# Cosformer attention and a quick-GELU MLP on one core: the last 64 rows of k and v on 64 partitions with zeroed rows below, instead of packed on two partition halves

## The chip, the cores and the metric

The kernel runs on one core of a Trainium2 chip. The metric is the device time of one execution in microseconds: 302.57 us for the kernel before, the median of 3 runs (302.42 to 303.06). The profile is a separate execution on the same kind of core; its span is 300.8 us.

TensorE multiplies matrices into PSUM, VectorE and ScalarE prepare operands and copy results out of PSUM, GpSimd issues most of the loads and stores, and SyncE issues the transposes by DMA.

## What is computed

Linear attention with cosine weights, and then a two-layer MLP over all tokens:

```python
# q, k, v: 8 batches, 8 heads, 576 positions, 64 columns
def phi(x, c, s):
    r = np.maximum(x, 0.0)
    return np.concatenate([r * c, r * s], axis=-1)      # 128 columns
q_p, k_p = phi(q, cos_w, sin_w), phi(k, cos_w, sin_w)
kv  = np.einsum('bhsf,bhsd->bhfd', k_p, v)              # per head: (128 x 576) (576 x 64)
z   = np.sum(k_p, axis=2)
num = np.einsum('bhsf,bhfd->bhsd', q_p, kv)
den = np.einsum('bhsf,bhf->bhs', q_p, z)[..., None] + 1e-06
x   = (num / den), as 4608 tokens of 512
h   = x @ w_in                                          # 512 -> 2048
out = (h * sigmoid(1.702 * h)) @ w_out                  # 2048 -> 512, float32
```

The kernel computes in bf16 with sums in f32. It takes z along as a 65th column of v that holds ones.

## The kernel before

The 4608 tokens are nine blocks of 512. In block i TensorE does the two MLP products of its tokens (the first is L305, into `mm` tiles; the second L345), and between them the attention of batch i + 1: q' and k' are prepared on VectorE, k^T v is computed per head (`unit_kv`), then the products of q' with it (`unit_num`, L289), and the result is turned by DMA into `xT` for the next block.

The sum over the 576 positions is cut into chunks of rows on partitions. Batches 0 and 1 use six chunks of 96 rows. Batches 2 to 7 use four chunks of 128 rows and a tail of 64, chunk 4. The tail is packed: heads 0 to 3 lie on partitions 0 to 63, heads 4 to 7 on partitions 64 to 127.

```python
def load_tail(b, n, on=nc.gpsimd):
    if n == "q":
        t = state[b][n, 4] = two.tile([64, 512], BF16, name=n + "t")
        on.dma_start(out=t.rearrange("p (h d) -> p h d", h=H),
                     in_=SRC[n][b, :, 512:576, :].rearrange("h p d -> p h d"))
        return
    t = state[b][n, 4] = two.tile([128, 256], BF16, name=n + "t")
    for m in range(2):
        on.dma_start(out=t[64 * m:64 * m + 64].rearrange("p (h d) -> p h d", h=4),
                     in_=SRC[n][b, 4 * m:4 * m + 4, 512:576, :].rearrange("h p d -> p h d"))
# ... (cut)
def kv_half(b, n, kv):                                   # L250; batch 1
    r, last = (96, 5) if b < 2 else (128, 4)
    for h in range(4 * n, 4 * n + 4):
        for c in range(last + 1):
            nc.tensor.matmul(kv[:, ds(h % 4 * (D + 1), D + 1)], kp[:r, c, h, :], vt[:r, c, h, 0:D + 1],   # L254
                             start=(c == 0), stop=(c == last))

def kv_tiled(b, kv):                                     # L257; batches 2 to 7
    for h in range(4):
        o = [kv[:, n, ds(h * (D + 1), D + 1)] for n in range(2)]
        for n in range(2):
            for c in range(4):
                nc.tensor.matmul(o[n], kp[:, c, h + 4 * n, :], vt[:, c, h + 4 * n, 0:D + 1],              # L263
                                 start=(c == 0), stop=False)
        for n in range(2):
            r = slice(64 * n, 64 * n + 64)
            nc.tensor.matmul(o[n], kp[r, 4, h, :], vt[r, 4, h, 0:D + 1], start=False, stop=True)          # L266
# ... (cut)
def unit_kv(b):
    kvs_new(b)
    kv = at_tile()                                       # two PSUM banks, one for each half n
    if b < 2:
        for n in range(2):
            kv_half(b, n, kv[:, n])
    else:
        kv_tiled(b, kv)
    for n in range(2):
        kvs_half(b, n, kv[:, n])                         # L269: copy on VectorE to bf16
# ... (cut)
def mm2_last(i, t):                                      # the last 128 tokens
    yps = mm_tile()
    ysb = ypool.tile([128, d_model], F32, name="ysb")
    for n in range(2):
        cols = slice(0, 384) if n == 0 else slice(384, 512)
        w = 384 if n == 0 else 128
        if n == 1:
            yps = mm_tile()
        for fc in range(FC):
            nc.tensor.matmul(yps[:, 0:w], gT[fc][:, ds(t * 128, 128)], w_out_sb[:, fc, cols],             # L369
                             start=(fc == 0), stop=(fc == FC - 1))
        if n == 0:
            nc.scalar.copy(ysb[:, cols], yps[:, 0:w])                                                     # L372
        else:
            nc.vector.tensor_copy(ysb[:, cols], yps[:, 0:w])                                              # L374
        # ... (cut: two stores of 64 rows each, one from SyncE, one from ScalarE, L376)
# ... (cut)
warmup(11, mm_tile())        # L463: eleven idle matmuls between the last transposes of q' and batch 0's first k^T v
kv_lo, kv_hi = mm_tile(), mm_tile()
kv0(kv_lo, 0, 4)
```

Of the kernel before, what the change touches and what calls it, by code (L numbers as in the profile page):

```python
# [9 lines left out]
F32 = mybir.dt.float32  # L10
BF16 = mybir.dt.bfloat16
# [10 lines left out]
def kernel(  # L22
# [9 lines left out]
    nc = tc.nc  # L32
    B, H, S, D = q.shape
    d_model = H * D
# [9 lines left out]
    one = ctx.enter_context(tc.tile_pool(name="one", bufs=1))  # L44
    two = ctx.enter_context(tc.tile_pool(name="two", bufs=2))
# [8 lines left out]
    def rows(c):  # L54
        return 128 if c < 4 else 64

    def wide(b, n):
        return b < 2 and n != "q"

    def krows(b, c):  # L60
        return 96 if b < 2 else 128

    warm = const.tile([128, TB], BF16)
    nc.vector.memset(warm, 0.0)
# [13 lines left out]
    state = {b: {} for b in range(B)}  # L78
    SRC = {"q": q, "k": k, "v": v}
# [7 lines left out]
                     in_=SRC[n][b, h0:h1, 0:np_ * t, :].rearrange("h (p c) d -> p h (c d)", c=t))  # L87

    def load_tail(b, n, on=nc.gpsimd):
        if n == "q":  # L90
            t = state[b][n, 4] = two.tile([64, 512], BF16, name=n + "t")
            on.dma_start(out=t.rearrange("p (h d) -> p h d", h=H),
                         in_=SRC[n][b, :, 512:576, :].rearrange("h p d -> p h d"))
            return

        t = state[b][n, 4] = two.tile([128, 256], BF16, name=n + "t")
        for m in range(2):
            on.dma_start(out=t[64 * m:64 * m + 64].rearrange("p (h d) -> p h d", h=4),  # L98
                         in_=SRC[n][b, 4 * m:4 * m + 4, 512:576, :].rearrange("h p d -> p h d"))

    def load_all(b):
        for n in "qkv":
# [4 lines left out]
    w_out_sb = one.tile([128, FC, d_model], BF16)  # L107
# [9 lines left out]
    pos_i = const.tile([128, NC], I32)  # L117
# [4 lines left out]
    for n in range(2):  # L122
        nc.sync.dma_start(out=q0[:, ts(n, 1024)].rearrange("p (h e) -> p h e", h=4),
                          in_=q[0, 4 * n:4 * n + 4, 0:512, :].rearrange("h (p c) d -> p h (c d)", c=4))
    nc.gpsimd.iota(pos_i[:, 0:4], pattern=[[1, 4]], base=0, channel_multiplier=4)
    for m in range(2):
        nc.gpsimd.iota(pos_i[64 * m:64 * m + 64, 4:5], pattern=[[1, 1]], base=512, channel_multiplier=1)
    nc.gpsimd.iota(pos6_i, pattern=[[1, 6]], base=0, channel_multiplier=6)
    load_main(0, "k", 0, 4)
    nc.gpsimd.iota(id_i, pattern=[[1, 128]], base=0, channel_multiplier=-1)  # L130
# [31 lines left out]
    kp = one.tile([128, 6, H, 2 * D], BF16, name="kp")  # L162
    vt = one.tile([128, 6, H, VW], BF16, name="vt")
# [22 lines left out]
    def part(b, n, c, h0, h1):  # L186
        if wide(b, n):
            return state[b][n][:96, 0:48 * D].rearrange("p (h c d) -> p c h d", c=6, d=D)[:, c, h0:h1]
        if c == 4 and n != "q":
            return state[b][n, 4].rearrange("p (h d) -> p h d", d=D)  # L190
        if c == 4:
            return state[b][n, 4].rearrange("p (h d) -> p h d", d=D)[:, h0:h1]
        return state[b][n][:, 0:32 * D].rearrange("p (h c d) -> p c h d", c=4, d=D)[:, c, h0:h1]
# [7 lines left out]
    def qn_slot(b, c):  # L201

        return state[b]["qn4"] if b < 2 and c == 4 else state[b]["qn"][:rows(c), c]

    def prep(b, n, c, h0=0, h1=H, on=(nc.vector, nc.vector)):
        r = rows(c) if n == "q" else krows(b, c)
        for cs, w in enumerate((cos6, sin6) if wide(b, n) else (cosw, sinw)):
            o = qn_slot(b, c) if n == "q" else kp[:r, c]
            if n == "k" and c == 4 and b > 1:
                h1 = 4  # L210
            oc, i, wc = o[:, h0:h1, cs * D:cs * D + D], part(b, n, c, h0, h1), w[:r, c:c + 1]
            if on[cs] is nc.scalar:
                nc.scalar.activation(oc, i, AF.Relu, scale=wc)
            else:
                nc.vector.tensor_scalar(oc, i, 0.0, wc, op0=MAX, op1=MUL)  # L215
# [2 lines left out]
        nc.vector.tensor_copy(vt[:96, :, :, 0:D], state[b]["v"][:96, 0:48 * D].rearrange("p (h c d) -> p c h d", c=6, d=D))  # L218

    def prep_v(b, c, h0=0, h1=H):  # L220
        if c == 4:
            h1 = 4
        nc.vector.tensor_copy(vt[:krows(b, c), c, h0:h1, 0:D], part(b, "v", c, h0, h1))

    def q_slot(b, c):
# [24 lines left out]
    def kv_half(b, n, kv):  # L250
# [3 lines that stand above are left out]
                nc.tensor.matmul(kv[:, ds(h % 4 * (D + 1), D + 1)], kp[:r, c, h, :], vt[:r, c, h, 0:D + 1],  # L254
                                 start=(c == 0), stop=(c == last))

    def kv_tiled(b, kv):  # L257

        for h in range(4):
            o = [kv[:, n, ds(h * (D + 1), D + 1)] for n in range(2)]  # L260
            for n in range(2):
                for c in range(4):
                    nc.tensor.matmul(o[n], kp[:, c, h + 4 * n, :], vt[:, c, h + 4 * n, 0:D + 1], start=(c == 0), stop=False)  # L263
            for n in range(2):
                r = slice(64 * n, 64 * n + 64)
                nc.tensor.matmul(o[n], kp[r, 4, h, :], vt[r, 4, h, 0:D + 1], start=False, stop=True)  # L266

    def kvs_half(b, n, kv, copy=nc.vector.tensor_copy, w=D + 1):
        copy(state[b]["kvs"][:, n, :, 0:D + 1],  # L269
             kv[:, 0:4 * w].rearrange("p (h e) -> p h e", h=4)[:, :, 0:D + 1])  # L270
# [4 lines left out]
    def unit_kv(b):  # L275
        kvs_new(b)
        kv = at_tile()
        if b < 2:
            for n in range(2):
                kv_half(b, n, kv[:, n])  # L280
        else:
            kv_tiled(b, kv)
        for n in range(2):
            kvs_half(b, n, kv[:, n])

# [15 lines left out]
    gT = {}  # L301
# [57 lines left out]
    def mm2_last(i, t):  # L359

        yps = mm_tile()
        ysb = ypool.tile([128, d_model], F32, name="ysb")
        for n in range(2):
            cols = slice(0, 384) if n == 0 else slice(384, 512)
            w = 384 if n == 0 else 128
            if n == 1:
                yps = mm_tile()
            for fc in range(FC):
                nc.tensor.matmul(yps[:, 0:w], gT[fc][:, ds(t * 128, 128)], w_out_sb[:, fc, cols],  # L369
                                 start=(fc == 0), stop=(fc == FC - 1))  # L370
            if n == 0:
                nc.scalar.copy(ysb[:, cols], yps[:, 0:w])  # L372
            else:
                nc.vector.tensor_copy(ysb[:, cols], yps[:, 0:w])  # L374
            for m, (p0, cnt, row, step) in enumerate(pieces(i * 4 + t)):
                (nc.sync if m == 0 else nc.scalar).dma_start(out=out[row:row + (cnt - 1) * step + 1:step, cols],  # L376
                                                             in_=ysb[p0:p0 + cnt, cols])
# [123 lines left out]
    for i in range(NBLK):  # L501
        work = {n: [] for n in range(32)}
        b = i + 1

        def at(n, f, *a):
            work[n].append(lambda: f(*a))

        if b < B:
            if i == 0:
                at(13, unit_num, 0, 4)  # L510
                at(13, turn_x, 0, 4)
            k0, k1, ks = (11, 24, (25, 26, 27, 28)) if i == 0 else (0, 12, (17, 19, 21, 23, 25))
            at(k0, prep_new, b)
            if i == 1:

                at(0, prep, 1, "q", 4)
                at(0, turn_q, 1, 4)
                at(14, unit_num, 1, 4)
                at(14, turn_x, 1, 4)
            for c in range(4 if i == 0 else NC):  # L520
                at(k0, prep, b, "q", c)
                if i == 0:
                    at(22 + c // 2, turn_q_at, b, c, AC.copy)
                else:
                    at(k0 + c, turn_q, b, c)
            for c in range(6 if b < 2 else NC):
                at(20 if i == 0 else k1 - 4 + c // 2, prep, b, "k", c)
                if b >= 2:
                    at(k1 - 1, prep_v, b, c)
            if b == 1:  # L530
                at(k1 - 1, prep_v_wide, b)
            at(k1, unit_kv, b)
            for c, k in enumerate(ks):
                at(k, unit_num, b, c)
                if i == 0 and c < 4:
                    at(min(k + 2, 31), turn_x_at, b, c)
                else:
                    at(k, turn_x, b, c)
            if 0 < i and b + 1 < B:
                at(1, load_all, b + 1)  # L540
        for n in range(32):
            if n < FC:
                if i > 0 or n > 3:
                    mm1(i, n)
            elif i == 0:
                mm2(i, n % 4, (n - FC) // 4)
            elif i == NBLK - 1 and n >= 28:
                if n == 28:
                    mm2_last(i, 3)
            else:  # L550
                mm2(i, (n - FC) // 4, n % 4)
            for f in work[n]:
                f()
        if i == 0:
            evac(i, 3, nc.vector)
# [30 lines left out]
```

## Time and profile before

| what | value |
|---|---|
| time, median of 3 | 302.57 us |
| span of the profile | 300.8 us |
| TensorE busy | 292.1 us, 97% |
| VectorE, ScalarE, GpSimd busy | 35%, 42%, 34% |
| memory traffic | 36.70 MB read, 9.44 MB written |
| L263, full-depth k^T v matmuls | 192, mean 194 ns |
| L266, half-depth k^T v matmuls | 48, mean 200 ns |
| L254, batch 1's k^T v matmuls, 96 rows | 48, mean 193 ns |
| L369, last tile | 16 of 384 columns, mean 326 ns; 16 of 128, mean 219 ns |

The page of a profile gives the busy time of each engine, the same in 40 slices of the span with the TensorE clock that was granted, the transfers, the chain of work that ended last, and the costliest groups of instructions. Groups are named by the line of the kernel. The mean of a TensorE group is the time from the start of one matmul to its end; matmuls follow each other before the one ahead has ended, so that the distance between two starts, and not the mean, says what one more of them costs. The timeline view gives these starts. A busy share of TensorE near 100% says that the engine always had a matmul under way, and not that it took them in at its best rate.

### The profile page before, as it was taken

To read this page: it belongs to the slowest core of one execution; us is meant where nothing else is said; L and a number is where in the kernel's file an instruction comes from. 1 tells how busy PE (TensorE), PEld (TensorE's weight loads), DVE (VectorE), ACT (ScalarE), POOL (GpSimd) and SP (SyncE) were. 2 spreads that over 40 slices of the span, in tenths; PEclk is the share of its full clock that TensorE was granted. 3 is DMA by queue.
4 is the path that set the end of the run, shared out by engine and by line. 5 is a ranking of instruction groups with operands and counts; after the bars stand their busy time and mean duration, and the time that the engine had idled before them with its cause. 6 is when DMAs were issued, how large, how long until landed. Compare 5 with 4: busy or idle time off the path is not lost.

```text
span 300.8 us, 5168 instructions
## 1 busy us (share of the span) xinstructions
PE 292.1 (97%) x1985; PEld 149.6 (50%) x1985; DVE 104.2 (35%) x355; ACT 126.1 (42%) x215; POOL 101.1 (34%) x130
## 2 busy tenths in 40 slices
PE   8979999999999999999999999999999999999994
PEld 3665456545544554455445544554455444444443
DVE  5740544663590159015811482147313300000000
ACT  7736622663137312641165116511652156226511
POOL 8532231550268025700691159003501110020021
PEclk9979999999999999999999999999999999999999
DMA  7999999599989987994899969996901520011033
GB/s 186 188 204 198 202 198 186 162 137 177 179 161 154 183 118 152 176 184 97 120 186 157 140 128 174 148 166 114 193 2 35 113 72 1 35 70 37 0 67 74
DMA packets 87496, 39.66 MB, mean 132 GB/s; under 512 B 57328, under 2 KB 85232, under 8 KB 87472
## 3 DMA queue, kind: packets, MB, share of 16 engines
q0 software_dynamic: 41040, 27.01, 59.9%
q1 hardware_dynamic: 46272, 12.20, 25.6%
q8 instruction: 15, 0.25, 0.3%
q10 hardware_dynamic: 160, 0.13, 0.1%
q14 instruction: 9, 0.07, 0.1%
HBM read 36.70 MB, written 9.44 MB: 153 GB/s over the span
## 4 chain that ended last, share of the span: by engine, by line
PE 93%; DVE 3%; ACT 1%; DMA 1%; issue 0%; DVEq 0%; ACTq 0%
PE mm L305 40%; PE mm L345 39%; PE at L289 3%; PE at L263 3%; PE mm L441 2%; DMA q<-in_q_dram 1%; PE mm L369 1%; DVE qn L215 1%; PE at L266 1%; PE mm L397 1%; PE mm L75 1%; DVE xb L297 1%; ACT qT L236 1%; ACT xT L435 1%; PE at L254 0%; PE mm L388 0%
## 5 line engine op out<-in xcount | busy, mean ns | idle before, releaser
L345 PE MATMUL mm<-w_out_sb,g 128*128 128x512 bf16 x560 | 128.6, 379 | 0.0
L305 PE MATMUL mm<-xT,w_in_sb 128*128 128x512 bf16 (+1 forms) x564 | 123.7, 378 | 0.0
L310 ACT ACTIVATE g<-mm 128x512 bf16<-128x512 f32 x144 | 85.5, 598 | 50.3 <-PE mm L305 49.8
L357 POOL DMA_DIRECT2D out_dram<-ysb x54 | 49.6, 922 | 163.3 <-ACT ysb L355 158.7
L305 PEld LDWEIGHTS <-w_in_sb 128*128 128x128 bf16 x564 | 54.3, 98 | 64.3 <-issue 0.2
L345 PEld LDWEIGHTS <-g 128*128 128x128 bf16 x560 | 52.2, 98 | 56.9
L355 ACT COPY ysb<-mm 128x512 f32<-128x512 f32 x34 | 19.9, 586 | 97.7 <-PE mm L345 97.7
L269 DVE CAST kvs<-at 128x260 bf16<-128x260 f32 x14 | 5.4, 425 | 66.6 <-PE at L266 59.6
L297 DVE TENSOR_TENSOR xb<-at,inv 128x512 bf16<-128x512 f32 (+1 forms) x36 | 24.8, 689 | 1.2
L295 DVE TENSOR_SCALAR den<-at 128x8 f32<-128x8 f32 (+1 forms) x36 | 5.9, 164 | 44.5 <-PE at L289 44.5
L374 DVE COPY ysb<-mm 128x128 f32<-128x128 f32 x1 | 0.3, 291 | 59.4 <-PE mm L369 59.4
L289 PEld LDWEIGHTS <-qT 128*128 128x128 bf16 x272 | 13.0, 98 | 8.2 <-DVE xb L297 0.6
L215 DVE TENSOR_SCALAR qn<-q,cosw 128x512 bf16<-128x512 bf16 (+1 forms) x36 | 12.5, 352 | 10.8 <-DMA q<-in_q_dram 10.8
L289 PE MATMUL at<-kvs,qT 128*128 128x65 bf16 x272 | 14.2, 194 | 0.3
L215 DVE TENSOR_SCALAR qn<-q,sinw 128x512 bf16<-128x512 bf16 (+1 forms) x34 | 12.6, 369 | 0.0
L98 POOL DMA_DIRECT2D vt<-in_v_dram x12 | 7.6, 641 | 7.8 <-DMA out_dram<-ysb 3.1
L98 POOL DMA_DIRECT2D kt<-in_k_dram x12 | 8.8, 749 | 4.1 <-DMA v<-in_v_dram 2.3
L263 PE MATMUL at<-vt,kp 128*128 128x65 bf16 x192 | 9.9, 194 | 0.0
L86 POOL DMA_DIRECT2D v<-in_v_dram x10 | 8.3, 834 | 4.4 <-DMA w_in_sb<-in_moe_w_in_dram 2.5
L215 DVE TENSOR_SCALAR kp<-k,sinw 128x512 bf16<-128x512 bf16 x24 | 8.9, 371 | 0.0
L86 POOL DMA_DIRECT2D k<-in_k_dram x9 | 7.8, 865 | 3.0 <-ACT g L310 2.5
L263 PEld LDWEIGHTS <-kp 128*128 128x128 bf16 x192 | 7.6, 97 | 2.1
(78 smaller groups left out, 155.7 us busy)
## 6 DMA issues: line engine op xcount, KB each, us to landing
out_dram<-ysb POOLq DMA_DIRECT2D x38, 128.0 KB, 3.0
out_dram<-ysb POOLq DMA_DIRECT2D x16, 256.0 KB, 3.0
q<-in_q_dram POOLq DMA_DIRECT2D x7, 512.0 KB, 10.3
k<-in_k_dram POOLq DMA_DIRECT2D x6, 512.0 KB, 11.5
v<-in_v_dram POOLq DMA_DIRECT2D x6, 512.0 KB, 12.3
w_out_sb<-in_moe_w_out_dram POOLq DMA_DIRECT2D x4, 512.0 KB, 18.2
w_in_sb<-in_moe_w_in_dram POOLq DMA_DIRECT2D x3, 512.0 KB, 12.4
q<-in_q_dram SPq DMA_DIRECT2D x2, 512.0 KB, 4.3
```

The lines of the kernel that those rows point to most:

```text
L86: on.dma_start(out=state[b][n][:np_, t * D * h0:t * D * h1].rearrange("p (h e) -> p h e", h=h1 - h0), in_=SRC[n][b, h0:h1, 0:np_ * t, :].r ...
L98: on.dma_start(out=t[64 * m:64 * m + 64].rearrange("p (h d) -> p h d", h=4), in_=SRC[n][b, 4 * m:4 * m + 4, 512:576, :].rearrange("h p d - ...
L215: nc.vector.tensor_scalar(oc, i, 0.0, wc, op0=MAX, op1=MUL)
L263: nc.tensor.matmul(o[n], kp[:, c, h + 4 * n, :], vt[:, c, h + 4 * n, 0:D + 1], start=(c == 0), stop=False)
L289: nc.tensor.matmul(nm[:, h // 4, ds(h % 4 * (D + 1), D + 1)], q_slot(b, c)[:, h, :], state[b]["kvs"][:, h // 4, h % 4, 0:D + 1], start=Tru ...
L297: nc.vector.tensor_tensor(state[b]["xb"][:r, c].rearrange("p (n h) d -> p n h d", n=2), nm4[:, :, :, 0:D], inv[:r].unsqueeze(3).to_broadca ...
L305: nc.tensor.matmul(hps[:, c0:c1], w_in_sb[:, kc, ds(fc * 128, 128)], xT[:, kc, ds(i * TB + c0, c1 - c0)], start=(kc == 0), stop=(kc == KC ...
L310: nc.scalar.activation(g, hps, AF.Gelu_apprx_sigmoid)
L345: nc.tensor.matmul(yps, gT[fc][:, ds(t * 128, 128)], w_out_sb[:, fc, :], start=(fc == 0), stop=(fc == FC - 1))
L355: nc.scalar.copy(ysb, cur[t])
L357: nc.gpsimd.dma_start(out=out[row:row + (n - 1) * step + 1:step, :], in_=ysb[p0:p0 + n, :])
L441: nc.tensor.matmul(first[fc][:, c0:c1], w_in_sb[:, kc, ts(fc, 128)], xT[:, kc, c0:c1], start=(kc == 0), stop=(kc == KC - 1))
```

## The change

The tails of k and v go back to 64 partitions, with all eight heads side by side, one load for each tail instead of two. Rows 64 to 127 of chunk 4 of k' and v are zeroed once, in block 1, and the product of batches 2 to 7 then takes chunk 4 at full depth like the other four: each head is five matmuls of 128 rows, and the half-depth pairs are gone. The heads are computed half by half, as in batch 1. The number of matmuls is the same. Apart from that, the last output tile is cut into two halves of 256 columns instead of 384 and 128, and one small table of positions is made by one instruction instead of two. The eleven idle matmuls ahead of batch 0's k^T v, which the change's name mentions, stand in both kernels.

What it is for: to rid the k^T v product of the two forms of matmul and of the packed layout, at the price of matmuls that multiply zeros.

```diff
     def krows(b, c):
-        return 96 if b < 2 else 128
+        return 96 if b < 2 else rows(c)
# ... (cut)
     def load_tail(b, n, on=nc.gpsimd):
-        if n == "q":
-            t = state[b][n, 4] = two.tile([64, 512], BF16, name=n + "t")
-            ...
-        t = state[b][n, 4] = two.tile([128, 256], BF16, name=n + "t")
-        for m in range(2):
-            on.dma_start(out=t[64 * m:64 * m + 64].rearrange("p (h d) -> p h d", h=4),
-                         in_=SRC[n][b, 4 * m:4 * m + 4, 512:576, :].rearrange("h p d -> p h d"))
+        if on is nc.gpsimd:
+            t = two.tile([64, 512], BF16, name=n + "t")
+        else:
+            t = one.tile([64, 512], F32, name=f"{n}t{b}")
+        state[b][n, 4] = t
+        on.dma_start(out=t.rearrange("p (h d) -> p h d", h=H),
+                            in_=SRC[n][b, :, 512:576, :].rearrange("h p d -> p h d"))
# ... (cut)
-    for m in range(2):
-        nc.gpsimd.iota(pos_i[64 * m:64 * m + 64, 4:5], pattern=[[1, 1]], base=512, channel_multiplier=1)
+    nc.gpsimd.iota(pos_i[:, 4:5], pattern=[[1, 1]], base=512, channel_multiplier=1)
# ... (cut: part, prep and prep_v lose their special cases for chunk 4)
-    def kv_tiled(b, kv):
-        ... (cut: the function shown above)
# ... (cut)
         kv = at_tile()
-        if b < 2:
-            for n in range(2):
-                kv_half(b, n, kv[:, n])
-        else:
-            kv_tiled(b, kv)
+        for n in range(2):
+            kv_half(b, n, kv[:, n])
# ... (cut)
+        hd = d_model // 2
         for n in range(2):
-            cols = slice(0, 384) if n == 0 else slice(384, 512)
-            w = 384 if n == 0 else 128
+            cols = ds(n * hd, hd)
# ... (cut: w becomes hd in the matmul and the two copies)
             if i == 1:
+                at(2, nc.vector.memset, kp[64:128, 4], 0.0)
+                at(2, nc.vector.memset, vt[64:128, 4], 0.0)
```

More of the change, by code (lines that the diff above doesn't have):

```diff
@@ L89, in load_tail @@
     def load_tail(b, n, on=nc.gpsimd):
-        if n == "q":
-            t = state[b][n, 4] = two.tile([64, 512], BF16, name=n + "t")
-            on.dma_start(out=t.rearrange("p (h d) -> p h d", h=H),
-                         in_=SRC[n][b, :, 512:576, :].rearrange("h p d -> p h d"))
-            return
-        t = state[b][n, 4] = two.tile([128, 256], BF16, name=n + "t")
-        for m in range(2):
-            on.dma_start(out=t[64 * m:64 * m + 64].rearrange("p (h d) -> p h d", h=4),
-                         in_=SRC[n][b, 4 * m:4 * m + 4, 512:576, :].rearrange("h p d -> p h d"))
+        if on is nc.gpsimd:
[5 more added lines that the diff above has]
+                            in_=SRC[n][b, :, 512:576, :].rearrange("h p d -> p h d"))
     def load_all(b):
@@ L188, in part @@
             return state[b][n][:96, 0:48 * D].rearrange("p (h c d) -> p c h d", c=6, d=D)[:, c, h0:h1]
-        if c == 4 and n != "q":
-            return state[b][n, 4].rearrange("p (h d) -> p h d", d=D)
         if c == 4:
@@ L208, in prep @@
             o = qn_slot(b, c) if n == "q" else kp[:r, c]
-            if n == "k" and c == 4 and b > 1:
-                h1 = 4
             oc, i, wc = o[:, h0:h1, cs * D:cs * D + D], part(b, n, c, h0, h1), w[:r, c:c + 1]
@@ L220, in prep_v @@
     def prep_v(b, c, h0=0, h1=H):
-        if c == 4:
-            h1 = 4
         nc.vector.tensor_copy(vt[:krows(b, c), c, h0:h1, 0:D], part(b, "v", c, h0, h1))
@@ L255, in kv_half @@
                                  start=(c == 0), stop=(c == last))
-    def kv_tiled(b, kv):
-        for h in range(4):
-            o = [kv[:, n, ds(h * (D + 1), D + 1)] for n in range(2)]
-            for n in range(2):
[L262 to L266, printed above, removed]
     def kvs_half(b, n, kv, copy=nc.vector.tensor_copy, w=D + 1):
@@ L277, in unit_kv @@
         kv = at_tile()
-        if b < 2:
-            for n in range(2):
-                kv_half(b, n, kv[:, n])
-        else:
-            kv_tiled(b, kv)
+        for n in range(2):
+            kv_half(b, n, kv[:, n])
         for n in range(2):
@@ L368, in mm2_last @@
             for fc in range(FC):
-                nc.tensor.matmul(yps[:, 0:w], gT[fc][:, ds(t * 128, 128)], w_out_sb[:, fc, cols],
+                nc.tensor.matmul(yps[:, 0:hd], gT[fc][:, ds(t * 128, 128)], w_out_sb[:, fc, cols],
                                  start=(fc == 0), stop=(fc == FC - 1))
             if n == 0:
-                nc.scalar.copy(ysb[:, cols], yps[:, 0:w])
+                nc.scalar.copy(ysb[:, cols], yps[:, 0:hd])
             else:
-                nc.vector.tensor_copy(ysb[:, cols], yps[:, 0:w])
+                nc.vector.tensor_copy(ysb[:, cols], yps[:, 0:hd])
             for m, (p0, cnt, row, step) in enumerate(pieces(i * 4 + t)):
```

## The prediction

> **What bounds the kernel now.** I read the busy share in slices first, then the chain that ended last, then TensorE's timeline at the two kinds of k^T v, then the last microseconds. From the page: busy tenths of TensorE in 40 slices, the granted TensorE clock, and the chain by engine and by line:
>
> ```profile
> PE   8979999999999999999999999999999999999994
> ...
> PEclk9979999999999999999999999999999999999999
> ...
> PE 93%; DVE 3%; ACT 1%; DMA 1%; issue 0%; DVEq 0%; ACTq 0%
> PE mm L305 40%; PE mm L345 39%; PE at L289 3%; PE at L263 3%; PE mm L441 2%; DMA q<-in_q_dram 1%; PE mm L369 1%; DVE qn L215 1%; PE at L266 1%; PE mm L397 1%; PE mm L75 1%; DVE xb L297 1%; ACT qT L236 1%; ACT xT L435 1%; PE at L254 0%; PE mm L388 0%
> ```
>
> After the third slice (some 23 us) TensorE is always busy, the clock is full, and the chain runs through TensorE for 93% of the span. The waits of TensorE agree: five groups of them, 4.1 us in all, none before L263, L266, L289 (the q'·kv products), L305 or L345. So every nanosecond taken off the TensorE stream after about 53 us comes off the time, unless a wait takes its place. The two lines the change touches, L263 and L266, are 4% of the chain together. What lies inside them is in the timeline of TensorE (start us, duration us, group), here batch 2's k^T v:
>
> ```profile
> 67.06 0.59 PE L305 MATMUL mm<-xT,w_in_sb 128*128 128x512 bf16 x2
> 67.50 0.41 PE L263 MATMUL at<-vt,kp 128*128 128x65 bf16 x8
> 67.83 0.20 PE L266 MATMUL at<-vt,kp 64*128 64x65 bf16 x2
> 67.97 0.42 PE L263 MATMUL at<-vt,kp 128*128 128x65 bf16 x8
> 68.32 0.20 PE L266 MATMUL at<-vt,kp 64*128 64x65 bf16 x2
> 68.45 0.41 PE L263 MATMUL at<-vt,kp 128*128 128x65 bf16 x8
> 68.80 0.20 PE L266 MATMUL at<-vt,kp 64*128 64x65 bf16 x2
> 68.94 0.42 PE L263 MATMUL at<-vt,kp 128*128 128x65 bf16 x8
> 69.28 0.20 PE L266 MATMUL at<-vt,kp 64*128 64x65 bf16 x2
> 69.42 0.39 PE L305 MATMUL mm<-xT,w_in_sb 128*128 128x512 bf16 x1
> ```
>
> The durations are latencies that overlap; the starts are what counts. Forty matmuls take from 67.50 to 69.42: 1.92 us (1.925 to 1.927 us in all six batches, from the single starts in the trace). For comparison the same stretch of batch 1, which has 48 matmuls in 96-row chunks and no half-depth ones:
>
> ```profile
> 46.21 1.61 PE L254 MATMUL at<-vt,kp 96*128 96x65 bf16 x48
> ...
> 47.66 0.60 PE L345 MATMUL mm<-w_out_sb,g 128*128 128x512 bf16 x2
> ```
>
> Here 48 matmuls take 47.66 - 46.21 = 1.45 us, 30.2 ns each. At that rate forty would take 1.21 us. The single starts say where the other 0.71 us is: from the last full-depth matmul to the first half-depth one 123 to 125 ns pass, the two halves start 3 to 4 ns apart, and 132 to 134 ns pass until the next full-depth matmul, against 29 to 35 ns between full-depth ones. The halves do run side by side, but each entry into and exit from them costs about 100 ns more than a plain step, four times in a batch.
>
> **What the Trainium skill says.** "TensorEngine Tiling (Array Packing)", section "Tiling Modes", Key Properties: "Changing tiling mode (not just tile) drains the TensorE". The trace agrees: 124 and 132 ns at the two changes. "TensorE: Matmul & The Clock Gate", section "Part 3: Packing small matmuls — row/col tiling", puts starts of neighbouring tiles about 4 ns apart; measured here 3 to 4 ns. Its section "Back-to-back issue gap" gives N/2.4 + 2.5 ns for N columns: 29.6 ns for 65 columns (here 29 to 35), 162.5 for 384 (here 160 to 163) and 55.8 for 128 (here 56). For 256 columns, which the new last tile needs and no row at full clock shows, I take an estimate from that formula: 109 ns.
>
> **The change, part by part.**
>
> *k^T v of batches 2 to 7.* Removed per batch: 32 full and 8 half-depth matmuls with eight changes of mode, 1.926 us. Added: 40 full-depth ones at 30.2 ns, 1.208 us. Gain 0.718 us. The first L305 matmul after the block is followed after 226 ns where the later ones are 216 apart; those 10 ns should go too. Six batches: 6 x 0.728 = 4.37 us, all on TensorE's stream.
>
> *VectorE.* Chunk 4 of k' and v was 128x256 (301 and 273 ns for k', 213 for v). Now it is 64x512, whose rows for q' and for v say 398, 339 and about 283 ns: 0.23 us more per batch. Once, in block 1, two memsets join: 64 rows of 512 and of 264 words; a 128x256-word one took 272 ns, so about 0.54 + 0.28 = 0.82 us. For batch 2 VectorE ended its preparation at 65.26 us, 2.2 us before the first k^T v; 1.05 us more still leaves 1.2. For batch 3 it ended at 89.56 and the product began at 98.58. Nothing of this reaches the path.
>
> *Loads.* Two issues per tail become one: 12 fewer in six batches, at 749 and 641 ns some 8 us of GpSimd's queue, which has room. Bytes and row size are the same. One iota fewer (126 ns) at the start lets k's load begin about 0.15 us earlier; TensorE does not wait for k there (eleven idle matmuls fill the time before its first product), so zero.
>
> *The last tile.* TensorE before: 16 x 162.5 + 16 x 55.8 = 3.49 us. After: 32 x 109 = 3.49 us, the same. What follows the last matmul changes:
>
> ```profile
> 296.17 0.48 ACT L372 COPY ysb<-mm 128x384 f32<-128x384 f32 x1 [2.01 <-PE mm L369]
> 296.67 1.19 SPq L376 DMA_DIRECT2D out_dram<-ysb  x2
> 296.68 1.46 ACTq L376 DMA_DIRECT2D out_dram<-ysb  x2
> 297.07 0.29 DVE L374 COPY ysb<-mm 128x128 f32<-128x128 f32 x1 [59.42 <-PE mm L369]
> ```
>
> VectorE's copy grows from 128 to 256 columns. Between 291 ns (128 columns) and 690 (512, at the end of block 0) a straight line gives 424: +0.13 us. The last two stores carry 64 KB each instead of 32, in rows of 1 KB: perhaps 0.1 us more. Against that, the first pair leaves about 1.0 us earlier; before, the second pair's packets began (298.61 and 298.80) just as the first pair's ended (298.54 and 298.83), so it may have queued. Net +0.15 us, half a guess.
>
> *Sum.* -4.37 + 0.15 = -4.2 us on the page's span and on the time.
>
> **Rivals.**
>
> 1. A wait on batch 2's q' transposes eats part of the gain. SyncE issued the five of them slowly, amid a crowded memory system:
>
> ```profile
> 60.02 16.13 SPq L229 DMA_TRANSPOSE qT<-qn  x5
> ```
>
> From issues and landing times I get landings near 74.9, 77.5, 78.4 and 80.4 us for chunks 1 to 4; their products start at 75.98, 77.96, 79.94 and 81.92. Chunk 2 has only 0.4 us to spare, and TensorE will come 0.7 us earlier, so up to 0.3 us may be lost, once. For it speaks the crowding; against it, two tail issues fewer in the very stretch of those transposes. In batch 3 the transposes are issued by 93 us for products at 104.84, so it does not recur. I put in 0.2 us.
>
> 2. The half-depth pairs are cheaper than full matmuls, and the change gives that back. Were a change of mode free, the pair would cost about 33 ns instead of 60, and undoing it would cost 4 x 27 ns x 6 = 0.65 us: 303.4 with the tail. The 124 and 132 ns steps speak plainly against it; batch 1's even 30.2 ns speaks for the new form.
>
> 3. Another engine or the memory becomes the bound, and the time stays at 302 to 302.6. ScalarE is busy 42%, VectorE 35%; memory is crowded up to 225 us, yet VectorE waited for q loads only twice, in the first 50 us, and TensorE for no transfer. Shortening a 31 us block by 0.7 us is 2%: too little to turn this round.
>
> 4. The start shifts against the clock throttle. The clock was half from 18.4 to 21.8 us. TensorE's stream up to there is unchanged, but a small shift of the loads could add or spare up to half of such a stretch, 1.7 us. I give this a tenth of the weight, either way.
>
> **Range and chances.** 302.57 - 4.2 + 0.2 = 298.6 us, 1.3% faster. The k^T v sum is measured on both sides and should hold to 0.3 us; tail and transposes together are uncertain by 0.3; run-to-run spread (302.42 to 303.06) and the clock widen the range upward and downward: 297.8 to 299.9. Faster by over 2% would need 296.5 or less, 2 us beyond the sum: 0.03. Slower by over 2% has no mechanism: 0.01.
>
> **What would show it.** The k^T v stretch of each of batches 2 to 7 should have 40 matmuls at 29 to 35 ns and 1.2 us from first to next stage; block length from one k^T v to the next should fall from 30.83 to about 30.1 us. The q'·kv products of batch 2 near 77 us would show a wait, or not. The time from the last matmul to the end should grow by 0.1 to 0.3 us. I would be wrong if full-depth steps stretched beyond 30 ns when the two banks are written one after the other, or if the gap before L305 stayed at 132 ns without a mode change.

## The result and the profile after

The changed kernel takes 298.56 us (median of four runs, 297.95 to 299.99) against 302.58 before (302.42 to 303.06): ratio 0.987, 95% interval 0.983 to 0.991. (Further down, a ratio to the kernel before and its interval stand in brackets.) The forecast was 298.6 us. Its span is 296.4 us, 4.4 less than before.

The page after the change, busy times and chain (busy us, share of the span, instructions; then shares by engine and by line):

```profile
PE 287.8 (97%) x1985; PEld 148.0 (50%) x1985; DVE 105.7 (36%) x357; ACT 126.1 (43%) x215; POOL 94.8 (32%) x117
...
PE 93%; DVE 3%; ACT 1%; DMA 1%; issue 0%; DVEq 0%; ACTq 0%
PE mm L281 41%; PE mm L321 40%; PE at L265 3%; PE at L244 3%; PE mm L417 1%; DMA q<-in_q_dram 1%; PE mm L345 1%; DVE qn L207 1%; PE mm L373 1%; PE mm L75 1%; DVE xb L273 1%; ACT qT L226 1%; ACT xT L411 1%; PE mm L364 0%; PE at L225 0%
```

Lines moved up by 10 to 24: L281 was L305, L321 was L345, L265 was L289, L345 was L369, and L244 holds all of k^T v in batches 1 to 7. TensorE is still busy for 97% and still the chain; it has the same 1985 matmuls, and 4.3 us less of busy time. Batch 2's k^T v in TensorE's timeline (start us, duration us, group):

```profile
66.89 0.59 PE L281 MATMUL mm<-xT,w_in_sb 128*128 128x512 bf16 x2
67.32 1.37 PE L244 MATMUL at<-vt,kp 128*128 128x65 bf16 x40
68.53 0.59 PE L281 MATMUL mm<-xT,w_in_sb 128*128 128x512 bf16 x2
```

One group of 40 stands where there were eight, and 68.53 - 67.32 = 1.21 us where there were 1.92. In the single starts the six batches take 1.205 to 1.210 us, with no step above 35 ns. From batch 3 on, 30.10 us pass from one k^T v product to the next; before, it was 30.83. The end of the kernel:

```profile
290.85 0.37 ACT L348 COPY ysb<-mm 128x256 f32<-128x256 f32 x1 [1.16 <-PE mm L345]
291.25 2.28 SPq L352 DMA_DIRECT2D out_dram<-ysb  x2
291.25 2.31 ACTq L352 DMA_DIRECT2D out_dram<-ysb  x2
292.61 0.42 DVE L350 COPY ysb<-mm 128x256 f32<-128x256 f32 x1 [59.42 <-PE mm L345]
```

VectorE's last copy takes 425 ns instead of 291. From the start of the last matmul to the end of the span it is 4.16 us, 4.04 before. And the waits have a new line (engine and line waiting, releaser: us in total, times, longest):

```profile
PEld L265 <- DMA qT<-qn: 0.8, 3, 0.4
```

Weight loads of q' waited for its transposes. On the matmuls only 75 ns of it shows in this profile, ahead of batch 2's third product near 77 us, where the step is 291 ns instead of 216.

### The profile page after: what moved, and what is told of

Same layout as the page of the kernel before. It is cut to its first block, busy times and chain, and to the rows that moved or that the text cites. A ratio compares the mean times of both kernels' runs of the same rounds, so it can differ in the third digit from the quotient of the medians.

```text
span 296.4 us, 5145 instructions
## 1 busy us (share of the span) xinstructions
PE 287.8 (97%) x1985; PEld 148.0 (50%) x1985; DVE 105.7 (36%) x357; ACT 126.1 (43%) x215; POOL 94.8 (32%) x117
## 4 chain that ended last, share of the span: by engine, by line
PE 93%; DVE 3%; ACT 1%; DMA 1%; issue 0%; DVEq 0%; ACTq 0%
PE mm L281 41%; PE mm L321 40%; PE at L265 3%; PE at L244 3%; PE mm L417 1%; DMA q<-in_q_dram 1%; PE mm L345 1%; DVE qn L207 1%; PE mm L373 1%; PE mm L75 1%; DVE xb L273 1%; ACT qT L226 1%; ACT xT L411 1%; PE mm L364 0%; PE at L225 0%
## 5 line engine op out<-in xcount | busy, mean ns | idle before, releaser
L321 PE MATMUL mm<-w_out_sb,g 128*128 128x512 bf16 x560 | 128.6, 379 | 0.0
L281 PE MATMUL mm<-xT,w_in_sb 128*128 128x512 bf16 (+1 forms) x564 | 123.6, 377 | 0.0
L333 POOL DMA_DIRECT2D out_dram<-ysb x54 | 50.7, 943 | 173.7 <-ACT ysb L331 172.3
L281 PEld LDWEIGHTS <-w_in_sb 128*128 128x128 bf16 x564 | 54.4, 98 | 64.1 <-issue 0.2
L321 PEld LDWEIGHTS <-g 128*128 128x128 bf16 x560 | 52.2, 98 | 56.9
L265 PEld LDWEIGHTS <-qT 128*128 128x128 bf16 x272 | 12.9, 98 | 8.3 <-DMA qT<-qn 0.8
L265 PE MATMUL at<-kvs,qT 128*128 128x65 bf16 x272 | 14.2, 194 | 0.3
L86 POOL DMA_DIRECT2D v<-in_v_dram x10 | 9.1, 920 | 5.2 <-DMA w_in_sb<-in_moe_w_in_dram 2.7
L244 PEld LDWEIGHTS <-kp 128*128 128x128 bf16 (+1 forms) x288 | 9.6, 97 | 1.6
L244 PE MATMUL at<-vt,kp 128*128 128x65 bf16 (+1 forms) x288 | 9.8, 193 | 0.0
L207 DVE TENSOR_SCALAR kp<-k,cosw 128x512 bf16<-128x512 bf16 x24 | 8.4, 350 | 0.0
L207 DVE TENSOR_SCALAR kp<-k,sinw 128x512 bf16<-128x512 bf16 x24 | 8.1, 337 | 0.0
L272 DVE RECIPROCAL inv<-den 128x8 f32<-128x8 f32 (+1 forms) x36 | 7.2, 201 | 1.2
```

The source lines that it names most:

```text
L86: on.dma_start(out=state[b][n][:np_, t * D * h0:t * D * h1].rearrange("p (h e) -> p h e", h=h1 - h0), in_=SRC[n][b, h0:h1, 0:np_ * t, :].r ...
L265: nc.tensor.matmul(nm[:, h // 4, ds(h % 4 * (D + 1), D + 1)], q_slot(b, c)[:, h, :], state[b]["kvs"][:, h // 4, h % 4, 0:D + 1], start=Tru ...
L272: nc.vector.reciprocal(inv[:r], den[:r])
L281: nc.tensor.matmul(hps[:, c0:c1], w_in_sb[:, kc, ds(fc * 128, 128)], xT[:, kc, ds(i * TB + c0, c1 - c0)], start=(kc == 0), stop=(kc == KC ...
L321: nc.tensor.matmul(yps, gT[fc][:, ds(t * 128, 128)], w_out_sb[:, fc, :], start=(fc == 0), stop=(fc == FC - 1))
L333: nc.gpsimd.dma_start(out=out[row:row + (n - 1) * step + 1:step, :], in_=ysb[p0:p0 + n, :])
```

## The experiments

The first four take the k^T v product and the last tile apart; the rest follow the new wait. A visit is one stay at half depth, with the change into it and the change out of it. The table gives what each profile shows: the length of one k^T v product of batches 2 to 7, how long TensorE's matmuls waited for q' transposes in batch 2 (steps above 216 ns, added up), and the time from the last matmul's start to the end.

| kernel | k^T v, us | wait in batch 2, us | last matmul to end, us | time, us |
|---|---|---|---|---|
| before | 1.926 | 0 | 4.04 | 302.58 |
| after | 1.206 | 0.08 | 4.16 | 298.56 |
| halves without partner | 2.870 | 0.63 | 4.15 | 307.99 |
| halves by fours | 1.503 | 1.88 | 4.05 | 301.01 |
| full depth, banks in turn | 1.205 | 0.84 | 4.16 | 298.99 |
| before, even last tile | 1.926 | 0.50 | 4.15 | 302.92 |
| after, second profile | 1.206 | 0.42 | 4.15 | 298.92 |
| after, 384 and 128 columns | 1.206 to 1.210 | 2.01 | 4.05 | 300.17 |
| after, third profile (meant as loads late) | 1.206 | 1.95 | 4.16 | 300.02 |
| after, products later | 1.207 | 0 | 4.15 | 297.72 |
| after, fourth profile | 1.206 | 1.62 | 4.15 | 299.52 |
| before, products later | 1.925 | 0 | 4.05 | 302.40 |
| after, loads behind stores | 1.205 | 0 | 4.15 | 300.26 |

The first two times are those of the result. The others come from three later sessions: the next four rows from one, in which the kernel before had a median of 302.93 us, the three after them from a second (303.33), the last four from a third (303.13).

**Half depth without a partner.** The changed kernel with chunk 4 at 64 rows:

```diff
             for c in range(last + 1):
+                r = krows(b, c)                  # 64 for chunk 4 of batches 2 to 7
                 nc.tensor.matmul(kv[...], kp[:r, c, h, :], vt[:r, c, h, 0:D + 1], ...)
```

> The changed kernel, but chunk 4 of batches 2 to 7 taken at half depth again (64 rows on partitions 0 to 63), one head at a time and without a partner on the other half. My theory, that each change between full and half depth costs about 100 ns more than a plain step: eight heads with one visit each, 8 x (3 x 30.2 + 124 + 132) = 2.8 us for the 40 matmuls, 1.6 us a batch more than at full depth, and about 298.6 + 9.5 = 308 us. The rival, that the cost came from two halves running side by side into two banks: no partner, no cost, 1.21 us a batch and 298.6 us.

Measured 307.99 us (ratio to before 1.014, 1.009 to 1.019) and 2.87 us a batch:

```profile
67.45 2.94 PE L245 MATMUL at<-vt,kp 128*128 128x65 bf16 x40
70.32 0.60 PE L282 MATMUL mm<-xT,w_in_sb 128*128 128x512 bf16 x2
```

The view joins both depths in one group; 70.32 - 67.45 is the length. The single steps of a head are 29, 35, 30, 124 and 133 ns: 124 to 125 into the half-depth matmul, 132 to 134 out of it, with no second half anywhere near. Going side by side is not what costs; entering and leaving half depth is.

The weight loads (engine PEld) show where in a step the time lies. Here are the first ones of batch 2 in the kernel before, and all forty in the kernel after:

```profile
67.50 0.28 PEld L263 LDWEIGHTS <-kp 128*128 128x128 bf16 x7
67.83 0.10 PEld L266 LDWEIGHTS <-kp 64*128 64x128 bf16 x2
67.97 0.29 PEld L263 LDWEIGHTS <-kp 128*128 128x128 bf16 x8
```

```profile
67.11 1.46 PEld L244 LDWEIGHTS <-kp 128*128 128x128 bf16 x40
```

Between two full-depth matmuls the weight load starts 1 to 11 ns after the start of the matmul ahead, and some 30 ns ahead of its own. At a change of depth, in the kernel before as in this one, it starts 119 to 120 ns after the matmul ahead on the way in and 128 to 130 ns on the way out, and its own matmul follows within 4 to 5 ns. So the time is lost ahead of the weight load, which otherwise starts almost together with the matmul ahead.

**Half-depth pairs by fours.** The kernel before, with two heads' sums of both halves open in four banks:

```diff
-        for h in range(4):
-            # 4 full-depth chunks of heads h and h + 4, then their two halves
+        for h0 in (0, 2):
+            for h in (h0, h0 + 1):   # 4 full-depth chunks of h and h + 4 each
+                ...
+            for h in (h0, h0 + 1):   # then four halves in a row
+                ...
```

> The kernel before, but the half-depth pairs of two heads put next to each other (four sums open in four banks), so that a batch enters and leaves half depth 2 times instead of 4, with the same 40 matmuls. My theory (cost per change of depth): each visit costs about 170 to 180 ns whatever it holds, so 1.93 - 2 x 0.175 = 1.57 us a batch, and 302.6 - 2.1 = 300.5 us. The rival (cost per half-depth pair): 1.93 us a batch and 302.6 us.

Measured 301.01 us (0.993, 0.991 to 0.995) and 1.503 us a batch:

```profile
67.50 0.65 PE L263 MATMUL at<-vt,kp 128*128 128x65 bf16 x16
68.08 0.23 PE L268 MATMUL at<-vt,kp 64*128 64x65 bf16 x4
68.25 0.66 PE L263 MATMUL at<-vt,kp 128*128 128x65 bf16 x16
68.84 0.24 PE L268 MATMUL at<-vt,kp 64*128 64x65 bf16 x4
69.01 0.39 PE L314 MATMUL mm<-xT,w_in_sb 128*128 128x512 bf16 x1
```

Same matmuls, half the visits, and 0.42 us less; the estimate was 0.35. With the run before this gives the price. Against forty full-depth steps (1.206 us) a batch with eight visits of one half costs 1.664 us more, with four visits of a pair 0.720, with two visits of two pairs 0.297: 208, 180 and 149 ns a visit. A visit thus costs about 208 ns, and each pair in it gives back about 29 ns, the step that it saves by running side by side (the steps within a visit of two pairs are 3, 35 to 36 and 3 to 4 ns).

**Full depth with the banks in turn.**

```diff
-        for n in range(2):
-            kv_half(b, n, kv[:, n])
+        for h in range(4):
+            for n in range(2):
+                ...   # all chunks of head h + 4 * n at full depth
```

> The changed kernel with the heads in the order of before (0, 4, 1, 5 and so on, the two banks in turn). My theory: the order costs nothing, 1.21 us a batch, 298.6 us. The rival, that going back and forth between the banks was part of the cost: between 1.21 and 1.9 us a batch and up to 302.6 us.

Measured 298.99 us (0.986, 0.980 to 0.992) and 1.205 us: the order costs nothing.

**The last tile alone.** The kernel before with 256 and 256 columns:

```diff
-            cols = slice(0, 384) if n == 0 else slice(384, 512)
-            w = 384 if n == 0 else 128
+            cols = ds(n * 256, 256)
+            w = 256
```

> The kernel before with only the last output tile cut into 256 and 256 columns. My theory: TensorE's 32 matmuls of the tile take the same 3.49 us, and the end comes 0.1 to 0.3 us later after the last matmul than the 4.04 us of before: 302.7 us. The k^T v product stays at 1.926 us a batch. The rival, that part of the 4 us gain came from the last tile: under 302 us.

Measured 302.92 us (0.999, 0.997 to 1.001), so the last tile brings none of the 4 us. The time can't tell 0.1 us; the trace can. From the tile's first matmul to its last start are 3.384 us for 256 and 256 columns, 3.438 for 384 and 128, because the last matmul's own step is not in that; with it (109 and 56 ns) it is 3.49 us for both. After it come 4.15 instead of 4.04 us. This profile also showed 0.5 us of waiting for q' transposes, in a kernel with the k^T v of before.

**The changed kernel once more.** The unaltered program, to see what varies.

> The changed kernel once more, with more rounds, because its four runs spread over 2 us (297.95 to 299.99) where those of before spread over 0.6. I expect 298.5 us and k^T v products of 1.206 us. If the wait for batch 2's transposes of q' (75 ns in the first profile) is what varies from run to run, this profile shows another length of it; if it is a stretch of half clock that falls now inside and now outside the busy time, the wait stays within 0.1 us and the clock row differs.

Measured 298.92 us (0.986, 0.983 to 0.989), with a wait of 0.42 us in its profile. Of the six runs, the three with a mean granted clock of 0.994 took 298.81 to 300.24 us, the three with 0.998 or more 297.96 to 299.04. Both suspects vary.

**The old last tile in the changed kernel.**

```diff
-            cols = ds(n * hd, hd)
+            cols = slice(0, 384) if n == 0 else slice(384, 512)
+            hd = 384 if n == 0 else 128
```

> The changed kernel with the last tile cut into 384 and 128 columns as before, so that the k^T v change stands nearly alone. My theory: the end comes 0.1 to 0.2 us earlier than in the changed kernel, 298.4 us. If the first store of before really queued ahead of the second, the gain is nearer 0.1.

Measured 300.17 us (0.990, 0.987 to 0.992): 1.25 us slower than the changed kernel in the same session, against the forecast. The end is not the reason: from the last matmul to the end it is 4.05 us, 0.1 shorter, as foreseen. The profile has a wait of 2.0 us here instead (the bracket is the idle time ahead, and what ended it):

```profile
77.80 0.42 PE L265 MATMUL at<-kvs,qT 128*128 128x65 bf16 x8
78.05 1.89 PE L321 MATMUL mm<-w_out_sb,g 128*128 128x512 bf16 x8
81.78 0.43 PE L265 MATMUL at<-kvs,qT 128*128 128x65 bf16 x8 [1.85 <-DMA qT<-qn]
```

Five of its six runs also had the lower clock, against three of six. The comparison by time alone would have told a false story of the last tile.

**Loads late, an edit that did nothing.** Batch 3's loads were to move away from batch 2's transposes; the second kernel has the old last tile as well.

```diff
-                at(1, load_all, b + 1)
+                at(14 if i == 1 else 1, load_all, b + 1)
```

> The changed kernel with batch 3's loads issued about 11 us later in block 1 (after its 15th step instead of its 2nd), out of the way of batch 2's transposes of q'. My theory: the five transposes are issued in some 7 us instead of 15.6, TensorE's wait of 75 ns at 76.85 us goes, and the time is 298.4 us; if that wait is what spreads the runs, they lie within 0.6 us. The rival, that the transposes are slow by themselves there: the wait stays. A risk: batch 2's transposes of the result then meet the loads, and block 2 begins with a wait.

> Both of the two preceding edits, the version that should be the fastest of these: no wait in batch 2 and the shorter end. About 298.3 us, 0.2 below the changed kernel.

They took 300.02 us (0.990, 0.986 to 0.994) and 300.20 us (0.991, 0.988 to 0.994). GpSimd has no work of its own between these two steps, so the instructions of every engine are the same as without the edit, in the same order: the loads went out at 57 us as ever. The two are thus repeats of the two kernels just above. The profile of the first shows a wait of 1.95 us, and the identical program has now shown 0.08, 0.42 and 1.95 us. (The second's profile was taken in a run disturbed by a clock of 0.95 throughout, and is not read.)

**Products later.** Batch 2's products of q' with k^T v move back by 2.6 us, first in the changed kernel:

```diff
             k0, k1, ks = (11, 24, (25, 26, 27, 28)) if i == 0 else (0, 12, (17, 19, 21, 23, 25))
+            if i == 1:
+                ks = (20, 22, 24, 26, 28)
```

> The changed kernel with batch 2's products of q' and k^T v taken 3 steps (2.6 us) later in block 1. In eight profiles of kernels that have the products at the old place TensorE waited there between 0 and 2.2 us for the transposes of q', a different length each time. My theory: with 2.6 us more room the wait is gone or under 0.1 us, the time is 0.5 to 1 us below the changed kernel of the same call, and the runs spread less. The rival, that the transposes only move along or that the next block then waits for its own operands: no gain, and a new wait at the start of block 2.

> The changed kernel unaltered, to stand beside its neighbours on the same chip: 298.9 us, k^T v 1.206 us, a wait of anything from 0 to 2.2 us in batch 2.

> The kernel before with the same later products in block 1. If the wait is already there before the change (its first profile showed none, one of a near copy 0.5 us), this gains 0.3 to 0.7 us on the kernel before. If the wait is only brought about by the earlier arrival of TensorE after the change, it gains nothing.

The three stood side by side. Products later in the changed kernel: 297.72 us (0.981, 0.978 to 0.984). The changed kernel: 299.52 (0.987, 0.984 to 0.990), with a wait of 1.6 us in its profile. (The 2.2 us of the expectations is a whole step; less the 0.22 us that it takes without a wait, the longest is 2.0 us.) Products later in the kernel before: 302.40 (0.996, 0.994 to 0.998), with its last tile and half-depth pairs as they were. All of TensorE's waits in the fastest of them, which has none for a transfer:

```profile
PE at L409 <- DVE xb L401: 1.4, 1, 1.4
PE at L75 <- DVE eps L151: 1.2, 1, 1.2
PE mm L417 <- ACT xT L411: 0.9, 2, 0.7
PE at L225 <- ACT qT L226: 0.3, 1, 0.3
PE at L382 <- ACT kvs L375: 0.3, 1, 0.3
PE mm L364 <- DVE qn L207: 0.2, 1, 0.2
```

With the wait gone the runs fall in two narrow groups by their clock. Medians, and the range in brackets:

| kernel | full clock (mean 0.998 or more) | lower clock (mean 0.995 or less) |
|---|---|---|
| before | 302.44 | 304.24 |
| before, products later | 301.18 (301.03 to 301.35) | 302.59 (302.21 to 302.82) |
| after | 298.66 (two runs) | 299.73 |
| after, products later | 296.91 (296.91 to 297.15) | 298.38 (298.29 to 298.56) |

(One run of the kernel before, at 0.994, took 302.46 us; the others of that group took 303.12 or more.) So the wait was in the kernel before too, where later products gain 1.26 us at full clock; its first profile, without a wait, was a lucky draw. In the changed kernel they gain 1.75. At the lower clock the gains are 1.65 and 1.35. Between the two kernels without the wait the difference is 301.18 - 296.91 = 4.27 us at full clock and 302.59 - 298.38 = 4.21 at the lower one; the steps in the trace say 4.38 for k^T v less 0.11 for the end, 4.27.

**Loads behind the stores.** The real move of batch 3's loads, behind the first two stores of block 1 in GpSimd's queue (`at(19 if i == 1 else 1, load_all, b + 1)`).

> The changed kernel with batch 3's loads put behind the first two stores of block 1 in GpSimd's queue, so that they start near 77 us instead of 58 us. (An earlier kernel that was meant to do this left the order of every queue as it was, so its loads went out at 57 us as ever.) If batch 3's loads are what makes batch 2's transposes slow, the five are issued in about 7 us instead of 15.6 and the wait is gone; VectorE will instead wait up to 3 us for q at the start of block 2, off the path. If the transposes are slow for another cause, the wait stays.

Measured 300.26 us (0.989, 0.985 to 0.993). SyncE's queue in the changed kernel of the session, and then here (start us, time over which the group was issued):

```profile
57.91 15.04 SPq L219 DMA_TRANSPOSE qT<-qn  x5
```

```profile
57.79 7.09 SPq L219 DMA_TRANSPOSE qT<-qn  x5
70.72 12.19 SPq L236 DMA_TRANSPOSE xT<-xb  x6
```

Without the loads beside them the five go out in 7.1 us, and TensorE's matmuls wait for none; in the profiles with the loads at the old place they take 15.0 to 16.4 us. So batch 3's loads are what slows batch 2's transposes. But the loads now lie on the transposes of the result, of which the last three land 8.4 to 9.9 us after their issue (2.3 to 4.2 us in the changed kernel), and the next blocks wait for those: two waits of 1.5 and 1.7 us in the steps between matmuls, the first of them here:

```profile
84.26 1.24 PE L321 MATMUL mm<-w_out_sb,g 128*128 128x512 bf16 x5
86.88 1.89 PE L281 MATMUL mm<-xT,w_in_sb 128*128 128x512 bf16 x8 [1.38 <-DMA xT<-xb]
```

Moving the consumer, 297.72 us, beat moving the loads. (In the profiles of this last session 35 of the 1985 matmul records are missing.)

## Why the prediction was right

**k^T v: right, to a few nanoseconds.** Forecast 1.208 us a batch and 10 ns more after it; measured 1.205 to 1.210, and the step after is 215 instead of 226 ns. Six batches: 6 x (1.926 - 1.207) + 6 x 0.011 = 4.38 us. The mechanism, a cost for each change of depth, is shown by three ways of visiting half depth (8, 4 and 2 visits a batch), and the two rivals for it, running side by side and the order of the banks, fell: the first kernel without partners was the slowest, and the alternating order was free. That a change of mode drains the array is what the Trainium skill says ("TensorEngine Tiling (Array Packing)", section "Tiling Modes", Key Properties); the held weight loads agree with it, and the runs give the price, but none shows what happens inside the array. Batch 1's 96-row matmuls show no such step among or around them (29 to 35 ns), so not every depth below 128 rows is a change of mode.

**No other bound: right.** TensorE is busy for 97% of the span as before, and waits for no engine that it did not wait for before; the one new wait is for the transposes.

**VectorE and loads: right.** Preparation for batch 2 ended at 66.13 us, before the product at 67.32. The memsets took 0.48 + 0.28 = 0.76 us (0.82 forecast). GpSimd ran 13 instructions fewer and was busy for 94.8 us instead of 101.1, 6.3 less, where some 8 was forecast. The iota was put at zero. The first profile after has batch 1's product 0.17 us earlier, but over all profiles that start lies between 44.8 and 46.8 us for both kernels alike, so nothing can be put down to it.

**The last tile: right.** TensorE's 3.49 us held, and the 256-column step of 109 ns. The end grew by 0.11 us, in all profiles with the even tile, where 0.15 was forecast; VectorE's copy took 425 ns where the straight line said 424. For the step of 256 columns the prediction took a formula from the Trainium skill ("TensorE: Matmul & The Clock Gate", section "Back-to-back issue gap"). The page means it for single, isolated matmuls, and for streams with a weight load before each matmul it has about 81 ns at 128 columns and 131 at 512; here, with a weight load for each, the steps are 56 and 216 ns, as the formula has it.

**The transposes: place and cause right, size left open.** "Up to 0.3 us may be lost, once", and 0.2 put in. The place and the cause were right: batch 2, the products of q', crowding. But the slack that the prediction computed from one profile is not a property of the kernel. Ten profiles with the products at the old place, the two first ones among them, show waits from 0 to 2.0 us, and the kernel before pays too. What counts is how much more the changed kernel pays, and that is the difference of the gains from later products: 1.75 - 1.26 = +0.5 us at full clock, but 1.35 - 1.65 = -0.3 us at the lower one, from two and four runs of the changed kernel. In the session before, with the loads-late repeat counted in, the medians of the two kernels differ by 3.4 us at full clock and 3.7 at the lower one; against the 4.2 to 4.3 us without the wait this leaves 0.9 and 0.5. So the runs neither confirm nor refute the 0.2 us. The first four runs of each kernel differed by 4.0 us; that they lie so near the forecast is in part luck of this wait.

**The clock: right to be in the range.** It was "a tenth of the weight". It deserved more: in the last session 13 of 25 runs of the kernel before and 4 of 6 of the kernel after had the lower clock, which costs 1.4 to 1.5 us where nothing else varies. The seven profiles with a stretch of half clock near 18 to 22 us have means of 0.992 to 0.994. It strikes both kernels, so it widens the range; a shift by the change is not shown.

**The span's sum.** -4.38 (k^T v) + 0.11 (end) + 0.08 (wait) - 0.17 (start) = -4.36 us, against 296.40 - 300.80 = -4.40.

## What to carry to other kernels

Half-depth matmuls packed on two partition halves pay only when many run in one visit: here a visit cost about 208 ns and a pair gave back about 29, so some seven pairs would be needed to break even (an estimate for these matmuls of 65 columns, from visits of two pairs at most), and padding 64 rows with zeros was cheaper by 0.72 us a batch. A slack read from one profile is one draw: the same wait was anything from 0.08 to 1.95 us in four profiles of one program. When a transfer lands in a crowded stretch, look at several profiles, or move its consumer as far back as is free, which gained 1.3 to 1.8 us here. And for effects of 0.1 us read the starts in the trace: two identical programs differed by 1.1 us in their medians.

## What the runs showed that was not expected

In these profiles, the moment at which the full clock began tells whether a stretch of half clock follows. In those of the kernels before and after, of the halves without partner and by fours, of the second profile after, of the old last tile in the changed kernel, and of products later in the kernel before, the full clock began 4.0 to 5.0 us after the start, and in each the half clock followed exactly 13.653 us later and lasted 3.413. In the other six that were read it began at 5.7 to 6.7 us, and no stretch followed. The rows of the granted clock in 40 slices show it, first of the kernel after, then of its version with products later:

```profile
PEclk9979999999999999999999999999999999999999
```

```profile
PEclk9999999999999999999999999999999999999999
```

The Trainium skill ("TensorE: Matmul & The Clock Gate", section "Part 1: The HAM clock gate") speaks of a window of 3413 ns that runs freely, whatever the start of the kernel; 13.653 us are four of them, and the stretch one. Near 16 us TensorE takes a step of 1.66 us, idle for 1.4 of them. In the fourth 3.41 us after the full clock began, TensorE is busy for 46 to 55% of the time in the seven profiles with the stretch and for 55 to 70% in the six without. That too little work there brings the half clock back would fit, but the two ranges touch, and no run tried it.
